# AFNO + SwiGLU block on one core: the first DFT takes rows that are not normalized

## The chip, the cores and the metric

The kernel runs on one core of a Trainium2 chip. The metric is device time in microseconds (us) of the whole program; smaller is better. The kernel before takes 1414.55 us (median of three runs, 1413.67 to 1416.0). Engine names below: PE multiplies matrices (TensorE), DVE is VectorE, ACT is ScalarE, POOL is GpSimd, SP (SyncE) issues most DMA transfers.

## The reference, cut to what matters

```python
x = A_x                                              # 4096 rows of 640
mod = (silu(c) @ w_mod)                              # sa, ca, ga, sb, cb, gb: 640 each
h = layernorm(x) * (1 + ca) + sa
x = x + ga * afno(h)          # rfft2, a two-layer complex MLP by 4 blocks of 160, soft shrink, irfft2
h = layernorm(x) * (1 + cb) + sb
x = x + gb * swiglu(h)        # 640 -> 1728 -> 640
```

The change touches only the first steps: the layer norm of x (each row minus its mean, times its reciprocal deviation) and the first half of the Fourier transform. The factor 1 + ca and the rest of the transform come right behind them.

## The kernel before, in words

The 4096 rows are laid out as 128 partitions (index n1) times 32 (index n2). Eight tiles xa0 to xa7 hold four n2 each: a tile is 128 partitions x 4 rows x 640. The 640 columns are four blocks of 160, each cut into 128 and a remainder of 32.

For each tile the kernel runs these steps. DVE computes statistics (`layer_stats`, L193 and L195), POOL turns them into 1/deviation `rs` (L197, L198) and -mean/deviation `nm` (L406, L407), and ACT (L418) and DVE (L416) together write the normalized rows in place (`ln_apply`). PE then multiplies by the constant DFT matrix `fa` over the partitions (`dft_a`, L439): five matmuls of 128x512 for a tile, one for the 128-wide parts of each row and one for the remainders of all four rows. They go through eight PSUM banks in rotation. ACT (L450, remainders L448) and for the last two tiles also DVE (L446) copy the result back into the same tile (`evac_a`).

The DFT's second half (`stage_b`, L600) needs, for a chunk of frequencies, all 32 n2 on the partitions. So the results are written to a scratch area in DRAM, s10 to s13, and read back as the chunk's tile `g` (`load_g`, L311). For the first chunk, g0, the last two tiles skip the scratch area: `move_g` (L316) copies their pieces from SBUF to SBUF, four transfers of 40 KB for each tile, half of them issued by SP and half by POOL. `moves(t)` is the list of transfers after tile t.

Beside this DVE forms the sum `acc0` of five rows of `w_mod` (`first_scale`, L428 and L430) that becomes the factor `ca1` after a product on PE (`columns`, L327). The first MLP weights w1 and the second ones w2 are each split into a high part (`weights_high`, POOL L281 and ACT L283) and a low part (`weights_low`, DVE L286, and `weights_rest`, POOL L528). The bias b2 is spread over all partitions by three products with ones (L481) and three copies on ACT (L487).

After `stage_b` of the first chunk, ACT and DVE write its parts z (L607, L608) and rz (L630, L640), and PE goes through the MLP: `stage_l1` (L661, L674), then `stage_l2` (L711), which needs the low parts of w1 and w2, the z and rz of each block, and r (L691).

The order on each engine is the order of the code (`manual_schedule`); a tile pool adds the waits. Each transfer reports its end on one of eight semaphores, DMAHW0 to DMAHW7 in the rows of the order below. They are handed out in turn, and a transfer first waits until the one that had its semaphore before has ended.

Of the kernel before, what the change touches and what calls it, by code (L numbers as in the profile page):

```python
# [6 lines left out]
F32 = mybir.dt.float32  # L7
# [6 lines left out]
P = 128  # L14
# [159 lines left out]
def body(tc, x, w1, b1, w2, b2, wg, wu, wd, c, wm, k_fa, k_tb, k_tx, k_bm, k_bx, k_ga, k_ge, k_id, out, dbg=None):  # L174
# [27 lines left out]
    with ExitStack() as top:  # L202
# [35 lines left out]
        with ExitStack() as af:  # L238
# [50 lines left out]
            af.enter_context(tc.manual_schedule())  # L289
            nc.sync.dma_start(fa, k_fa)  # L290
# [45 lines left out]
            stx = ExitStack()  # L336
            xp = stx.enter_context(tc.tile_pool(name="xp", bufs=1, side="right"))
            rp = af.enter_context(tc.tile_pool(name="rp", bufs=1))
            b2t = rp.tile([P, 2, NB, BS], F32, name="b2t")
            with tc.tile_pool(name="sp", bufs=1) as sp:  # L340
                xas = []
                xts = {t: xp.tile([P, 4, D], F32, name=f"xa{t}") for t in (1, 2, 3, 0, 4, 5, 6, 7)}

                def load_x(t):
                    xa = xts[t]
                    if t < 3:
                        for i in range(4):
                            nc.sync.dma_start(xa[:, i, :], xv[:, 4 * t + i, :])
                    else:
                        nc.sync.dma_start(xa, xv[:, 4 * t:4 * t + 4, :])  # L350
                    xas.append(xa)


                def write_s1(t, f):
                    nc.sync.dma_start(s1[f][4 * t:4 * t + 4].rearrange("n r d -> r n d"),
                                      xas[t][(slice(0, 64, 4), slice(64, P, 4), slice(2, P, 4), slice(1, P, 2))[f]])

                for t in range(6):
                    load_x(t)
                wm1 = sp.tile([P, 5, D], F32, name="wm1")  # L360
                stats = {}
                pas = {}
                raws = {}


                def moves(t):
                    if t < 6:
                        write_s1(t, 0)
                    if t < 4:
                        write_s1(t, 1)  # L370
                    if t == 0:
                        load_x(6)
                        nc.sync.dma_start(c5, c)
                    elif t == 1:
                        load_x(7)
                        raws[1] = load_weights(sp, w1, "1")
                    elif t == 2:
                        nc.sync.dma_start(wm1, wm[:, 1])
                    elif t == 3:
                        load_tb(0)  # L380
                        nc.sync.dma_start(b1m, b1[:, 0:8].rearrange("p (r b) -> p r b", r=2))
                        nc.sync.dma_start(b1r, b1[0:64, 8:12])
                        nc.sync.dma_start(b2s[0:1], b2.rearrange("r b o -> (r b o)").unsqueeze(0))
                    elif t == 4:

                        load_g(0, (0, 1))
                        raws[2] = load_weights(rp, w2, "2", (0,))
                    elif t == 5:
                        for f in (2, 3):
                            write_s1(1, f)  # L390
                    elif t == 6:

                        for i in range(4):
                            move_g(0, t, i, (pool, nc.sync)[i // 2])
                        load_g(0, (2,))
                    elif t == 7:
                        for i in range(4):
                            move_g(0, t, i, (pool, nc.sync)[i // 2])


                def ln_stats(t):
                    n = 1 if t < 2 else 4
                    for i in range(0, 4, n):
                        mv, rs = layer_stats(lp, xas[t][:, i:i + n, :], n, f"a{t}_{i}")
                        nm = lp.tile([P, 4], F32, tag="nm", bufs=7, name=f"nm{t}_{i}")
                        pool.tensor_tensor(nm[:, :n], mv[:, :, 0], rs, op=OP.mult)  # L406
                        pool.tensor_tensor(nm[:, :n], nm[:, :n], mone[:, :n], op=OP.mult)  # L407
                        for k in range(n):
                            stats[t, i + k] = (mv[:, k, 0:1], rs[:, k:k + 1], nm[:, k:k + 1])

                def ln_apply(t):
                    xa = xas[t]
                    for i in range(4):
                        mean, rs, nm = stats[t, i]
                        if i >= (4, 2, 2, 3, 2, 3, 2, 1)[t]:
                            dve.tensor_scalar(xa[:, i, :], xa[:, i, :], mean, rs, op0=OP.subtract, op1=OP.mult)  # L416
                        else:
                            act.activation(xa[:, i, :], xa[:, i, :], AF.Identity, bias=nm, scale=rs)  # L418


                b2s = sp.tile([P, 2 * NB * BS], F32, name="b2s")
                pool.memset(b2s, 0.0)
# [32 lines left out]
                for t in range(8):  # L455
                    if t + 2 < 8:
                        ln_stats(t + 2)
# [2081 lines left out]
```

## Time and profile before

| what | value |
|---|---|
| median of 3 runs | 1414.55 us |
| the profiled execution | 1411.32 us, its span 1409.5 us |
| PE busy over the span | 1382.5 us, 98% |
| DVE, ACT, POOL busy | 76%, 54%, 43% |
| first DFT (L439) on PE, first start to last end | 7.98 to 49.30 us |
| first matmul of `stage_b` (L600) | 55.84 us |
| last wait of PE in the first chunk's MLP (L711) ends | 70.20 us |

Times of rows count from the start of the span. A row of the timeline stands for a run of instructions of one line: its start, its length, the engine, line and operation, the tiles out<-in, the count, and in brackets the idle time of the engine before it with what ended that. An f32 matmul is two instructions (x2) for one call in the code. "Idle before" says which engine or transfer came last.

### The profile page before, as it was taken

The page shows a single profiled execution, that of the slowest core. Times are in us where ns is not written, and L with a number is a line of the kernel's source. Part 1 is how long each engine was busy: PE and PEld are TensorE (multiplying, and loading weights), DVE is VectorE, ACT ScalarE, POOL GpSimd, SP SyncE. Part 2 cuts the span into 40 slices and gives each one's busy share as a digit, 9 for nine tenths or more (in the row PEclk, how much of TensorE's full clock was granted, in tenths as well). Part 3 has the DMA queues.
Part 4 walks back from the last instruction along what each step waited for, and adds up shares of the span by engine and source line. Part 5 has one row for each costly group of instructions (what it writes and reads, how often), then busy time and mean ns, then how long its engine had stood idle before and what let it go on. Part 6 is the DMA issues. An engine that isn't in the chain of part 4 may idle for free. (4 is left out here: it accounts for less than half of the span.)

```text
span 1409.5 us, 23754 instructions
## 1 busy us (share of the span) xinstructions
PE 1382.5 (98%) x8410; PEld 1310.7 (93%) x8410; DVE 1067.8 (76%) x1861; ACT 765.0 (54%) x1542; POOL 604.6 (43%) x683
## 2 busy tenths in 40 slices
PE   6899999999999999999999999999999999999998
PEld 2599999967999889899999999999999999999998
DVE  8889888889888888649787668678678757375644
ACT  6879999755555554436454345546164624262341
POOL 5700200157766594326445534447153624042241
PEclk9999999999999999999999999999999999999999
DMA  9876466675998897898877998696998668956634
GB/s 371 310 244 211 157 196 193 203 232 170 327 353 308 308 335 263 293 368 308 308 225 281 375 330 288 236 326 230 375 330 309 217 218 282 350 194 217 199 115 149
DMA packets 171016, 377.34 MB, mean 268 GB/s; under 512 B 22193, under 2 KB 81649, under 8 KB 168882
## 3 DMA queue, kind: packets, MB, share of 16 engines
q1 hardware_dynamic: 161794, 359.28, 73.6%
q0 software_dynamic: 6800, 13.93, 3.1%
q10 hardware_dynamic: 2304, 2.62, 0.5%
q8 instruction: 66, 1.08, 0.3%
q14 instruction: 52, 0.43, 0.1%
HBM read 269.48 MB, written 96.80 MB: 260 GB/s over the span
## 5 line engine op out<-in xcount | busy, mean ns | idle before, releaser
L1442 DVE TENSOR_TENSOR wb<-r,wb 128x768 fp32r<-128x768 f32 (+3 forms) x170 | 170.4, 1013 | 13.5 <-ACT wb L1435 13.3
L2050 PE MATMUL pw<-h,wt 128*128 128x384 f32 x412 | 139.3, 338 | 0.6 <-ACT s_y L2069 0.6
L2052 PE MATMUL pw<-h,wt 128*128 128x384 f32 x412 | 138.3, 336 | 0.0
L2051 PE MATMUL pw<-h,wt 128*128 128x384 f32 x412 | 138.1, 335 | 0.0
L1435 ACT ACTIVATE wb<-r 128x768 fp32r<-128x768 f32 (+3 forms) x168 | 104.5, 639 | 56.3 <-PE pw L2063 41.7
L2351 PE MATMUL pc<-wq,L 128*128 128x320 f32 x846 | 132.7, 309 | 0.9 <-DMA wq<-wqd 0.9
L2110 POOL TENSOR_TENSOR sg<-s_x,sg 128x384 f32<-128x384 f32 x24 | 30.0, 1250 | 234.5 <-DVE s_x L2076 234.5
L2351 PEld LDWEIGHTS pc<-wq,L 128*128 128x128 f32 x846 | 126.3, 188 | 1.1 <-DVE x L2308 1.1
L2130 DVE TENSOR_TENSOR L<-sg,L 128x384 fp32r<-128x384 f32 x144 | 101.0, 725 | 27.7 <-ACT L L2126 27.2
L2069 ACT ACTIVATE s_x<-pw 128x384 f32<-128x384 f32 x52 | 25.6, 492 | 164.2 <-PE pw L2052 162.3
L2050 PE MATMUL pw<-h,wb 128*128 128x384 f32 x312 | 105.0, 336 | 0.0
L2051 PE MATMUL pw<-h,wb 128*128 128x384 f32 x312 | 104.4, 335 | 0.0
L2052 PE MATMUL pw<-h,wb 128*128 128x384 f32 x312 | 104.4, 335 | 0.0
L2121 POOL TENSOR_TENSOR sg<-sg,sg 128x384 f32<-128x384 f32 x72 | 91.9, 1276 | 23.4 <-DVE L L2130 20.0
L1973 PE MATMUL pg<-ht,wb 128*128 128x512 f32 x260 | 101.8, 392 | 0.0
L2351 PE MATMUL pe<-wq,L 128*128 128x320 f32 x648 | 101.7, 309 | 0.0
L1974 PE MATMUL pg<-ht,wb 128*128 128x512 f32 x260 | 101.3, 390 | 0.0
L1975 PE MATMUL pg<-ht,wb 128*128 128x512 f32 x260 | 101.2, 389 | 0.0
L2267 PE MATMUL pd<-wq,a 128*128 128x320 f32 x632 | 96.8, 310 | 0.0
L2351 PEld LDWEIGHTS pe<-wq,L 128*128 128x128 f32 x648 | 96.6, 188 | 0.0
L2267 PEld LDWEIGHTS pd<-wq,a 128*128 128x128 f32 x632 | 93.5, 188 | 0.5
L772 POOL DMA_DIRECT2D s<-co x28 | 15.7, 559 | 175.9 <-ACT co L771 175.9
(317 smaller groups left out, 3914.1 us busy)
## 6 DMA issues: line engine op xcount, KB each, us to landing
wq<-wqd SPq DMA_DIRECT2D x83, 640.0 KB, 6.1
wt<-td SPq DMA_DIRECT2D x103, 512.0 KB, 5.4
hs<-ho SPq DMA_DIRECT2D x52, 512.0 KB, 5.2
h<-hs SPq DMA_DIRECT2D x32, 768.0 KB, 7.9
td<-wt SPq DMA_DIRECT2D x25, 512.0 KB, 6.3
r<-in_B_w_gate_dram SPq DMA_DIRECT2D x24, 384.0 KB, 4.4
r<-in_B_w_up_dram SPq DMA_DIRECT2D x24, 384.0 KB, 4.3
xx<-tt SPq DMA_DIRECT2D x56, 160.0 KB, 3.3
```

The lines of the kernel that those rows point to most:

```text
L1435: def high(ks, e=slice(0, c), copy=lambda o, i: act.activation(o, i, AF.Copy)):
L1442: dve.tensor_tensor(wbs[t, n][:, 1, ks, e], raw[t, n][:, ks, e], f32(wbs[t, n][:, 0, ks, e]), op=OP.subtract)
L1973: mm(b, wh, hh, start=(kk == 0), stop=False)
L1974: mm(b, wh, hl, start=False, stop=False)
L1975: mm(b, wl, hh, start=False, stop=(kk == 4))
L2050: mm(b, w(0, kp), a[:, kp, 0], start=start and kp == 0, stop=False, skip_group_check=not start)
L2051: mm(b, w(0, kp), a[:, kp, 1], start=False, stop=False, skip_group_check=not start)
L2052: mm(b, w(1, kp), a[:, kp, 0], start=False, stop=kp == 1, skip_group_check=not start)
L2121: pool.tensor_tensor(o, x, y, op=op)
L2130: dve.tensor_tensor(o[:, 1], raws[j], f32(o[:, 0]), op=OP.subtract)
L2267: mm(b[:, :320], l, m, start=start and i == 0, stop=stop and i == len(s) - 1)
L2351: mm(o[:, :320], ls[q][:, x, k], w[:, q, y], start=start and q == 0 and n == 0, stop=q == 1 and n == 2, skip_group_check=not start)
```

## The change

For tiles 1 to 6 the rows are no longer normalized before the DFT. Since the DFT runs over the partitions, and each partition has its own mean and deviation, the deviation can be multiplied into the matrix and the mean added behind it. (Line numbers in this section are those of the changed kernel.)

- `scaled` (L489, L491) writes for each row its own matrix wt = fa * rs, 128x128: rows 0 to 2 on ACT, row 3 on POOL (tile 1: all on ACT). The matmul of a row uses wt and the raw row (L527).
- A sixth matmul for each of these tiles, fa times the four columns `nm`, gives what the mean adds: a column of four values for each frequency. ACT copies it to `bt` (`bias_a`, L531), and the copies back from PSUM add it (ACT L543, for two rows of tile 6 DVE L539).
- The remainders of the four rows are still normalized (`rest`, ACT L498, DVE L500): 4x32 elements of each partition and row.
- Tile 0's rows stay normalized on ACT (L480), tile 7's on DVE (L482). Statistics from tile 2 on go in pairs of rows.

Beside that:

- c is loaded by the ACT queue at the start, and its Silu comes ahead of the first row (L421). 14 small matmuls on ones run on PE at the start (`idle(14)`, L422), and 6 instead of 4 behind `columns`.
- b2 is spread by one transfer of 640 KB (L616), behind tb1 on SP, in place of three products and three copies.
- The transfers: `move_g` of tile 6 goes wholly to SP, of tile 7 half to the ACT queue (rows 0 and 2 of the tile) and half to SP. The load of rm2 (the first part of w2) moves behind the writes to s12 and s13 of tile 1.
- The low parts of w1: the first one stands ahead of the last copy of tile 7 on DVE, five ahead of `ca1`, one behind it, and five (`prep1[7:]`) behind the z and rz of block 0.
- The code of `stage_b` and of the copies behind it moves ahead; rz lives in another pool.

```diff
             af.enter_context(tc.manual_schedule())
+            nc.scalar.dma_start(c5, c)
             nc.sync.dma_start(fa, k_fa)
...
                 def moves(t):
                     if t < 6:
                         write_s1(t, 0)
+                    else:
+                        for i in range(4):
+                            move_g(0, t, i, nc.scalar if t == 7 and i % 2 == 0 else nc.sync)
...
                     elif t == 4:
-
                         load_g(0, (0, 1))
-                        raws[2] = load_weights(rp, w2, "2", (0,))
                     elif t == 5:
                         for f in (2, 3):
                             write_s1(1, f)
+                        raws[2] = load_weights(rp, w2, "2", (0,))
                     elif t == 6:
-
-                        for i in range(4):
-                            move_g(0, t, i, (pool, nc.sync)[i // 2])
                         load_g(0, (2,))
-                    elif t == 7:
-                        for i in range(4):
-                            move_g(0, t, i, (pool, nc.sync)[i // 2])
...
+                def scaled(t, *rows):
+                    if t not in wts:
+                        wts[t] = sp.tile([P, 4, P], F32, tag="wt", bufs=2, name=f"wt{t}")
+                    for i in rows:
+                        if t > 1 and i == 3:
+                            pool.tensor_scalar(wts[t][:, i, :], fa, stats[t, i][1], None, op0=OP.mult)
+                        else:
+                            act.activation(wts[t][:, i, :], fa, AF.Copy, scale=stats[t, i][1])
+
+                def rest(t, *rows):
+                    for i in rows:
                         mean, rs, nm = stats[t, i]
...
+                        v = xas[t][:, i, :].rearrange("p (b e) -> p b e", b=NB)[:, :, 128:160]
+                        if i < 2:
+                            act.activation(v, v, AF.Identity, bias=nm, scale=rs)
                         else:
...
+                            dve.tensor_scalar(v, v, mean, rs, op0=OP.subtract, op1=OP.mult)
...
+                    for i in (4, 0, 1, 2, 3) if t == 7 else (0, 1, 2, 3, 4) if t == 0 else (0, 1, 2, 3, 5, 4):
+                        pa = pas[t, i] = bank_a(f"pa{t}_{i}")
+                        if i == 5:
+                            mm(pa[:, 0:4], fa, nms[t], start=True, stop=True)
+                        elif i == 4:
+                            mm(pa, fa, xnr[:, :, :, 128:160], start=True, stop=True)
+                        else:
+                            mm(pa, fa if plain else wts[t][:, i, :], xnr[:, i, :, 0:128], start=True, stop=True)
...
+                def bias_a(t):
+                    bts[t] = sp.tile([P, 4], F32, tag="bt", bufs=3, name=f"bt{t}")
+                    act.activation(bts[t], pas[t, 5][:, 0:4], AF.Copy)
...
+                        elif t == 6 and i % 2:
+                            dve.tensor_scalar(xa[:, i, 0:512], pas[t, i], bts[t][:, i:i + 1], None, op0=OP.add)
+                        elif t == 7 and i == 3:
                             dve.tensor_copy(xa[:, i, 0:512], pas[t, i])
+                        elif t in bts:
+                            act.activation(xa[:, i, 0:512], pas[t, i], AF.Identity, bias=bts[t][:, i:i + 1])
...
+                for t in range(2, 7):
+                    ln_stats(t + 1, A)
+                    rest(t, 2, 3)
+                    ln_stats(t + 1, B)
+                    if t < 6:
+                        scaled(t + 1, 3)
+                    scaled(t, 0, 1)
+                    bias_a(t - 1)
+                    rest(t, 0, 1)
+                    if t == 2:
+                        evac_a(1, 0, 1)
+                    scaled(t, 2)
+                    evac_a(t - 1, *((2, 3) if t == 2 else (0, 1, 2, 3)))
+                    evac_a(t - 1, 4)
                     dft_a(t)
...
+                    moves(t - 1)
...
+                for job in prep1[1:6]:
                     weights_low(*job)
+                dve.tensor_scalar(ca1, pm1[:, 0:5], 1.0, None, op0=OP.add)
...
+                nc.sync.dma_start(b2t.rearrange("p r b o -> p (r b o)"),
+                                  b2.rearrange("r b o -> (r b o)").unsqueeze(0).to_broadcast([P, 2 * NB * BS]))
...
+                weights_low(*prep1[6])
+                evac_b(0, 0)
+                evac_r(0, 0)
+                for job in prep1[7:]:
+                    weights_low(*job)
```

What it does to the order stands below at three places. First SP, from the load of rm2 to the load of rr2 (the second part of w2), before (rm2 is w2's first part, s10 to s13 the scratch areas, g0 the first chunk's tile, xa6 and xa7 the last two tiles; in brackets what a row waits for):

```order
L253 DMA rm2_456<-in_A_w2_dram 128x1280 [waits DMAHW5_49]
L355 DMA s10<-xa5_120 16x4x640 [waits DMAHW6_49,DVE_49,Activation_49]
L355 DMA s12<-xa1_115 32x4x640 [waits DMAHW7_49]
L355 DMA s13<-xa1_115 64x4x640 [waits DMAHW0_49]
L316 DMA g0_453<-xa6_121 4x4x640 [waits DMAHW1_49,Activation_49]
L316 DMA g0_453<-xa6_121 4x4x640 [waits DMAHW2_49,DVE_49]
L311 DMA g0_453<-s10 32x2560 [waits DMAHW6_49,DMAHW3_49]
L316 DMA g0_453<-xa7_122 4x4x640 [waits DMAHW4_49,Activation_49]
L316 DMA g0_453<-xa7_122 4x4x640 [waits DMAHW5_49,DVE_49]
L492 DMA rr2_457<-in_A_w2_dram 128x1280
```

The same stretch of SP after the change:

```order
L416 DMA s12<-xa1_116 32x4x640 [waits DMAHW7_49]
L416 DMA s13<-xa1_116 64x4x640 [waits DMAHW0_49]
L253 DMA rm2_595<-in_A_w2_dram 128x1280 [waits DMAHW1_49]
L317 DMA g0_541<-xa6_122 4x4x640 [waits DMAHW2_49,Activation_49]
L317 DMA g0_541<-xa6_122 4x4x640 [waits DMAHW3_49,DVE_49]
L317 DMA g0_541<-xa6_122 4x4x640 [waits DMAHW4_49]
L317 DMA g0_541<-xa6_122 4x4x640 [waits DMAHW5_49,DVE_49]
L312 DMA g0_541<-s10 32x2560 [waits DMAHW6_49]
L317 DMA g0_541<-xa7_123 4x4x640 [waits DMAHW7_49,Activation_49]
L317 DMA g0_541<-xa7_123 4x4x640 [waits DMAHW0_49,DVE_49]
L608 DMA rr2_596<-in_A_w2_dram 128x1280 [waits DMAHW1_49]
```

Two more moves of tile 6 stand on SP, and the load of rm2 now stands right ahead of all of them, with a wait on DMAHW1.

Second ACT, from the last copies of tile 7 to the first high parts of w1, after the change (before, the copy of xa7's remainders was followed by the high parts at once):

```order
L545 ACTIVATE xa7_123<-pa7_2_624 128x512 [waits PE_49]
L537 ACTIVATE xa7_123<-pa7_4_618 128x4x128 [waits DVE_49,PE_49]
L317 DMA g0_541<-xa7_123 4x4x640 [waits DMAHW1_49,Activation_49]
L317 DMA g0_541<-xa7_123 4x4x640 [waits DMAHW3_49]
L283 ACTIVATE w1a_92<-rm1_362 128x4x128 [waits DMAHW7_49]
L283 ACTIVATE w1b_93<-rm1_362 128x4x128
```

Two moves of tile 7 stand here now, on semaphores DMAHW1 and DMAHW3. In the numbering of the program each comes ahead of SP's transfer with the same semaphore: SP's load of rm2 waits for the count 80 of DMAHW1, which the first of these two moves brings it to, and SP's second move of tile 6 for the count 80 of DMAHW3, which the second one brings it to.

Third DVE, from the second six low parts of w1 (the first six stand ahead of them) to the low part of w2a, before (w1a, w1b, w1c are the parts of w1, pb_0 the PSUM of `stage_b`):

```order
L286 SCALAR_TENSOR_TENSOR w1a<-rm_320,w1a 128x4x128
L286 SCALAR_TENSOR_TENSOR w1b<-rm_320,w1b 128x4x128
L286 SCALAR_TENSOR_TENSOR w1c<-rr_321,w1c 128x4x128
L286 SCALAR_TENSOR_TENSOR w1a<-rm_320,w1a 128x4x32
L286 SCALAR_TENSOR_TENSOR w1b<-rm_320,w1b 128x4x32
L286 SCALAR_TENSOR_TENSOR w1c<-rr_321,w1c 128x4x32
L608 SCALAR_TENSOR_TENSOR z_0_663<-pb_0_646,ca_68,z_0_663 128x2x256
L640 SCALAR_TENSOR_TENSOR rz_666<-pb_4_651,ca_68,rz_666 32x256 x2
L608 SCALAR_TENSOR_TENSOR z_1_671<-pb_1_656,ca_68,z_1_671 128x2x256
L640 SCALAR_TENSOR_TENSOR rz_666<-pb_4_651,ca_68,rz_666 32x256 x2
L286 SCALAR_TENSOR_TENSOR w2a<-rm_456,w2a 128x4x160
```

After, from `ca1` on:

```order
L606 TENSOR_SCALAR ca_68<-pmc 128x5
L286 SCALAR_TENSOR_TENSOR w1a<-rm_362,w1a 128x4x128
L359 SCALAR_TENSOR_TENSOR z_0_734<-pb_0_716,ca_68,z_0_734 128x2x256
L391 SCALAR_TENSOR_TENSOR rz_737<-pb_4_721,ca_68,rz_737 32x256 x2
L286 SCALAR_TENSOR_TENSOR w1b<-rm_362,w1b 128x4x128
L286 SCALAR_TENSOR_TENSOR w1c<-rr_363,w1c 128x4x128
L286 SCALAR_TENSOR_TENSOR w1a<-rm_362,w1a 128x4x32
L286 SCALAR_TENSOR_TENSOR w1b<-rm_362,w1b 128x4x32
L286 SCALAR_TENSOR_TENSOR w1c<-rr_363,w1c 128x4x32
L359 SCALAR_TENSOR_TENSOR z_1_751<-pb_1_726,ca_68,z_1_751 128x2x256
L391 SCALAR_TENSOR_TENSOR rz_737<-pb_4_721,ca_68,rz_737 32x256 x2
L286 SCALAR_TENSOR_TENSOR w2a<-rm_595,w2a 128x4x160
```

Five low parts of w1 have moved from ahead of z of block 0 to between its rz and the z of block 1. From tb1 on (SP) and from the low part of w2a on (the other engines), the two programs have the same instructions in the same order, b2's transfer apart.

452 lines of the change are left out of this document (231 added, 221 removed).

## The prediction

> **What bounds the kernel now.** I read the page's busy times first, then busy time by stretches, then PE's timeline up to 75 us, and only then the other engines in the same stretch.
>
> ```profile
> PE 1382.5 (98%) x8410; PEld 1310.7 (93%) x8410; DVE 1067.8 (76%) x1861; ACT 765.0 (54%) x1542; POOL 604.6 (43%) x683
> ```
> ```profile
> 71.00:1409.50 1338.50, 1327.08 (x8214) 1280.49 (x8212) 1006.84 (x1703) 711.39 (x1449) 558.81 (x603) 1.00 0.77 264
> ```
>
> Behind 71 us PE is busy 1327.08 of 1338.50 us (the first two figures). Nothing that the change touches lies there, and there is almost no idle time to take up a delay. So what the change does to the moment from which PE runs without waits passes to the end nearly one to one. The question is when that moment comes.
>
> ```profile
> 7.98 9.09 PE L439 MATMUL pa<-xa,fa 128*128 128x512 f32 x14 [7.98 <-ACT xa L418]
> 17.78 11.97 PE L439 MATMUL pa<-xa,fa 128*128 128x512 f32 x26 [0.71 <-DVE xa L416]
> 31.56 17.74 PE L439 MATMUL pa<-xa,fa 128*128 128x512 f32 x40 [1.81 <-ACT xa L418]
> ...
> 51.13 2.40 PE L481 MATMUL pb<-b2s,ones 128*128 128x512 f32 x6
> 53.36 1.05 PE L334 MATMUL pz<-ones 128*128 128x128 f32 x8
> 55.84 2.92 PE L600 MATMUL pb<-tb,g 128*128 128x128 f32 x24 [1.43 <-DMA g<-xa]
> ...
> 69.28 0.38 PE L711 MATMUL pc<-w2c,r 128*128 128x320 f32 x1 [1.07 <-DVE r L691]
> 70.20 0.39 PE L711 MATMUL pc<-w2c,r 128*128 128x320 f32 x1 [0.53 <-DVE w2c L286]
> ```
>
> Three things are read here. The DFT ends at 31.56 + 17.74 = 49.30. Then PE has small work until 53.36 + 1.05 = 54.41 and waits 1.43 us, last for a transfer into g. And the last wait, at 70.20, is for DVE: the low part of w2c. Between 55.84 and 70.20 the chain runs over DVE:
>
> ```profile
> 55.13 0.68 DVE L286 SCALAR_TENSOR_TENSOR w1c<-rr,w1c 128x512 fp32r<-128x512 f32 x1
> 55.73 0.28 DVE L286 SCALAR_TENSOR_TENSOR w1a<-rm,w1a 128x128 fp32r<-128x128 f32 x1
> ...
> 57.73 0.75 DVE L608 SCALAR_TENSOR_TENSOR z<-pb,ca,z 128x512 fp32r<-128x512 f32 x1 [1.31 <-ACT z L607]
> 58.87 0.97 DVE L640 SCALAR_TENSOR_TENSOR rz<-pb,ca,rz 32x256 fp32r<-32x256 f32 x2 [0.40 <-ACT rz L630]
> 59.87 0.75 DVE L608 SCALAR_TENSOR_TENSOR z<-pb,ca,z 128x512 fp32r<-128x512 f32 x1
> 60.85 0.98 DVE L640 SCALAR_TENSOR_TENSOR rz<-pb,ca,rz 32x256 fp32r<-32x256 f32 x2 [0.23 <-ACT rz L630]
> 61.86 1.83 DVE L286 SCALAR_TENSOR_TENSOR w2a<-rm,w2a 128x640 fp32r<-128x640 f32 x1
> ...
> 69.16 0.89 DVE L286 SCALAR_TENSOR_TENSOR w2c<-rr,sgn,w2c 128x640 fp32r<-128x640 f32 x1
> ```
>
> From z at 57.73 to 70.05 DVE waits 0.40 and 0.23 us and no more. Whatever is put into that row delays w2c by its length.
>
> **Step 1: the DFT stage ends some 3 us sooner.** PE before needs 17.74 us for the last 20 calls, 0.887 each. Tiles 1 to 7 make 35 such calls, plus six products with four columns. No row shows such a product; the nearest is 24 instructions in 2.92 us in stage_b, 0.24 a pair, and I take 0.2. That is 35 x 0.887 + 6 x 0.2 = 32.2 us. Tile 1 cannot start before its deviations are there:
>
> ```profile
> 11.54 0.21 DVE L195 BATCH_NORM_AGGREGATE mv_a<-st_a 128x2 f32<-128x12 f32 x1
> ...
> 13.73 3.19 DVE L193 BATCH_NORM_STATS2 st_a<-xa 128x6 f32<-128x320 f32 x8
> 16.84 0.41 DVE L195 BATCH_NORM_AGGREGATE mv_a<-st_a 128x2 f32<-128x12 f32 x4
> 17.16 1.08 DVE L416 TENSOR_SCALAR xa<-xa,mv_a,rs_a 128x640 f32<-128x640 f32 x2
> ```
>
> Its second row's mean and variance are there at 11.75; with POOL and one ACT operation behind that (about 2 us) I take 13.9. So PE ends at 13.9 + 32.2 = 46.1, if nothing else holds it: 3.2 us sooner. DVE does not: a tile takes 3.19 + 0.41 and two short operations, about 4.0 us, under PE's 4.6. ACT is close:
>
> ```profile
> 37.05 2.06 ACT L450 ACTIVATE xa<-pa 128x512 f32<-128x512 f32 x4
> 38.95 0.64 ACT L448 ACTIVATE xa<-pa 128x512 f32<-128x512 f32 x1
> 39.43 1.78 ACT L418 ACTIVATE xa<-xa,nm,rs_a 128x640 f32<-128x640 f32 x2
> ...
> 49.34 0.60 ACT L448 ACTIVATE xa<-pa 128x512 f32<-128x512 f32 x1 [0.26 <-PE pa L439]
> ...
> 51.39 0.30 ACT L283 ACTIVATE w1a<-rm 128x128 fp32r<-128x128 f32 x1
> ```
>
> A tile costs it four copies (2.06, or with a bias at most four times 0.8 x 0.89 = 2.85), the remainders' copy (0.64), three 128x128 of wt and two of rest (0.2 to 0.3 each) and bt (about 0.2): 3.9 to 5.2 us, against PE's 4.6. I take PE as the bound and give ACT's upper end to a rival. The products for b2 (2.40), three copies on ACT and the moves that POOL issued cost nothing where they stood, since PE, ACT and POOL waited for g behind them; their going gives nothing.
>
> **Step 2: SP stands still and gives the 3 us back.** SP reaches the load of rm2 early, but that row waits for the semaphore's earlier user, which is ACT's move of tile 7. That move is issued only behind ACT's last copy. With PE 3.2 us sooner, ACT's end at 49.94 becomes 46.5 or so. Until this move has landed, SP issues nothing: not tile 6's four moves, not load_g, not tile 7's two. The transfers have these times (median us from issue to landing, then minimum, median and maximum of all into g):
>
> ```profile
> out_dram<-x ACTq DMA_DIRECT2D x12, 160.0 KB, 1.8
> ```
> ```profile
> g<-s SPq DMA_DIRECT2D x3, 320.0 KB, 4.3
> ...
> g<-xa POOLq DMA_DIRECT2D x4, 40.0 KB, 5.0
> ```
> ```profile
> DMA to landing us min/median/max: 3.4/4.8/5.6
> ```
> ```profile
> 46.65 1.61 SPq L316 DMA_DIRECT2D g<-xa  x2
> 50.14 0.53 SPq L311 DMA_DIRECT2D g<-s  x1
> 50.76 1.20 SPq L316 DMA_DIRECT2D g<-xa  x2
> ```
>
> The move's landing takes 1.8 us (ACT's own queue) to 5.0 us (moves of this size, from POOL). SP's earlier writes will by then have had several us to drain, so I take 2.2: rm2 goes at 48.7. Behind it 0.6 for rm2 and four moves at 0.6 put load_g at 51.7, against 50.14 before; with 4.3 us it lands at 56.0. Tile 7's last move goes at 52.9 and lands at about 55.5. rm2 itself is later too, and ACT splits w2a from it (1.36) ahead of z:
>
> ```profile
> 53.88 1.36 ACT L283 ACTIVATE w2a<-rm 128x640 fp32r<-128x640 f32 x2
> ```
>
> A load of this size took 8.4 us at worst (row further down), which gives 48.7 + 8.4 + 1.4 = 58.5 for z, where step 4 has z at 58.1: covered but for 0.4. Before, stage_b began at 55.84. It will begin near 56.1: **+0.3 us**, with -0.9 (1.8 us for the move, 3.4 for load_g; tile 7's last move then ends it) and +4 (5.0 and 5.6, which give 4.1) as ends. The Trainium skill (DMA: Bandwidth & Descriptors, on arbitration) says that each DMA engine takes packets from its queues in turn, which speaks for the short end: a move on ACT's queue would not wait behind all of SP's. No row here shows it.
>
> **Step 3: five low parts in DVE's chain.** Before, they stood at 54.53 to 56.42, while DVE waited for z anyway. Now they stand between rz and z of the next block: from the rows 0.6 + 0.6 (0.68 less the overlap) and three times 0.2, together 1.85 us. The wait of 0.23 ahead of the second rz goes. That is **+1.6**. If POOL's weight work beside it slows them as it slows w2a (1.83 against 0.89 for w2c of the same size), it is up to +3; but then w2a and w2b come when POOL is further on, and win back as much.
>
> **Step 4: PE runs slow after the wait.** After step 1 PE is done with its six small products near 49 us and has nothing until 56.1: 7 us idle, where before it was 1.43. What idle time does is shown only at the program's start, behind 7.98 us without work:
>
> ```profile
> L439 PE MATMUL pa<-xa,fa x6: 1061/1061/1222, 8.0 to 12.4; 128*128 128x512 f32 x6
> ```
> ```profile
> L439 PE MATMUL pa<-xa,fa x72: 592/592/807, 13.3 to 47.9; 128*128 128x512 f32 x72
> ```
>
> The first matmuls take 1061 ns (median of minimum, median, maximum), those from 13.3 us on 592. If PE begins slow again, stage_b's 24 instructions take 2.92 x 1061/592 = 5.2 us in place of 2.92. The first rz needs 16 of them, +1.55; behind that the low parts of step 3 cover the rest. Ends: 0 and +1.55, and 2.3 if nothing covers it. I take **+1.3**. The Trainium skill (TensorE: Matmul & The Clock Gate, Part 1) has the rule: PE's clock falls to half after an idle window of about 3.4 us and is whole again after about as long at work. By it the 7 us will slow PE here; without it the sum would be +1.9.
>
> The spread of b2 (640 KB) goes behind tb1 and is needed first by DVE's add:
>
> ```profile
> 65.69 0.57 SPq L298 DMA_DIRECT2D tb<-in_k_tb_dram  x1
> ```
> ```profile
> 73.38 0.89 DVE L713 TENSOR_TENSOR tt<-pc,b2t 128x320 f32<-128x320 f32 x2
> ```
> ```profile
> rm<-in_A_w_dram SPq DMA_DIRECT2D x2, 640.0 KB, 8.4
> ```
>
> tb1's issue at 65.69 moves by the 1.6 us that load_g moved, so b2's goes at 67.9 and, taking 8.4 like the first parts of w1 and w2 of the same size, lands at 76.3; the add comes at 73.38 + 3.2 = 76.6. No wait, with little to spare.
>
> The sum: 0.3 + 1.6 + 1.3 = **+3.2 us**. The profiled execution (1411.32 = span 1409.5 + 1.8) is 3.2 under the median; the sum is added to the median: 1414.55 + 3.2 = **1417.75 us**.
>
> **The rivals.**
> - No slow PE. If only step 2 and 3 hold, +0.3 + 1.6 = +1.9: 1416.5. For it: no row shows a slow PE in mid-program. Against: the start does, after as long a pause.
> - It ends faster: the hold on SP does not bite, because the semaphore's count is reached some other way. Then tile 6's moves and load_g go before 46 us, tile 7's moves at 46.5 to 47.7, and g is whole near 50.5, 5.3 us sooner. PE's pause is 2 us. Less step 3: -3.7, so 1410.9. It decides if stage_b starts before 52. Against it stands the order of the rows themselves.
> - A longer hold. ACT binds the DFT (5.2 us for a tile, +0.6 on each of five) or the move lands late: ACT's move comes 2 to 3 us later, and all behind it: +5.2 to +6.2, 1420.3.
> - The change does not do what it says: the DFT ends at 49 as before since ACT's added work is as long as PE's. Then the hold costs its full 3.2 more: +6.4, 1421. I count it with the last one.
>
> **How the numbers follow.** Chances: the sum as it stands 0.55, no slow PE 0.20, a longer hold 0.13, no hold 0.12. About 0.2%, 2.8 us, is what a measurement of this kernel tells from no change. Over +2.8 lie 0.40 of the first case (its terms reach from +2 to +5), a tenth of the second and all of the third: slower 0.55. Within it lie 0.15 and 0.18 of the first two: same 0.33. Faster: 0.12. The range: below 1412.6 most of the case without a hold is left out, and above 1421.5 the worst of the third case (+3.5 of hold, 1.85 and 1.55 make 6.9, 1421.45; the hold's far end of 4 is left out). The likeliest case alone reaches from 1416.5 to 1419.5.
>
> **What would show it.** Step 1: PE's last DFT matmul ends near 46. Step 2: SP's queue shows a gap of some 5 us ahead of rm2, ended by ACT's move of tile 7, and stage_b starts at 56. Step 3: five low parts between rz and z at about 61, and w2c's end 3 us later, near 73. Step 4: L600's instructions at 500 ns in place of 275. The forecast is too slow if stage_b starts before 52, too fast if after 58, and wrong in its frame if PE has new waits behind 80 us.

## The result, and the profile after

| | before | after |
|---|---|---|
| median of 4 runs | 1415.09 us (1413.67 to 1416.0) | 1424.05 us (1422.71 to 1424.53) |
| ratio, with 95% interval | 1 | 1.0063 [1.0045, 1.008] |
| profiled execution, its span | 1411.32, 1409.5 us | 1422.71, 1420.9 us |
| last DFT matmul ends | 49.30 us | 47.76 us |
| first matmul of `stage_b` | 55.84 us | 59.74 us |
| last wait of PE in the first MLP ends | 70.20 us | 76.22 us |

The change makes the kernel 9.0 us slower (median against median). The forecast, 1417.75, was in the right direction and a third of the size (3.2 us); the time lies above the range. The two profiled executions differ by more, 11.4 us, since the one of before is among that kernel's shorter ones.

The busy time of PE in the page of the kernel after, and its granted clock by stretches (columns: PE, PEld, DVE, ACT, POOL busy, the clock, DMA share, GB/s):

```profile
PE 1388.6 (98%) x8448; PEld 1318.8 (93%) x8448; DVE 1065.8 (75%) x1863; ACT 764.1 (54%) x1561; POOL 603.3 (42%) x695
```
```profile
50.00:60.00 10.00, 1.23 (x10) 1.07 (x9) 2.25 (x7) 3.63 (x8) 4.49 (x3) 0.81 0.70 205
60.00:73.00 13.00, 10.78 (x74) 10.09 (x73) 9.27 (x17) 8.11 (x17) 7.05 (x7) 0.88 0.96 331
```

PE's 98% hides the place: from 50 to 60 us it works 1.23 us, and up to 73 us at a clock of 0.88. Its timeline after, at the rows that the prediction named:

```profile
42.16 1.12 PE L525 MATMUL pa<-xa,fa 128*128 128x512 f32 x2 [0.67 <-DVE xa L482]
...
45.78 1.98 PE L527 MATMUL pa<-xa,fa 128*128 128x512 f32 x4 [0.78 <-DVE xa L539]
...
49.39 1.58 PE L335 MATMUL pz<-ones 128*128 128x128 f32 x12
59.74 4.47 PE L351 MATMUL pb<-tb,g 128*128 128x128 f32 x24 [8.77 <-DMA rr<-in_A_w_dram]
...
76.22 0.39 PE L790 MATMUL pc<-w2c,r 128*128 128x320 f32 x1 [0.54 <-DVE w2c L286]
```

The DFT ends at 45.78 + 1.98 = 47.76. Small products follow until 49.39 + 1.58 = 50.97, then an idle time of 8.77 us ahead of `stage_b` (L351 now). The row names rr2's load, the transfer issued last; what L351 reads is tb and g, so the moves into g are what it must wait for (this trace shows no landing of its own for them). Where these moves stand is in the queues of SP and of ACT:

```profile
42.13 1.92 SPq L416 DMA_DIRECT2D s<-xa  x3
50.71 0.34 SPq L253 DMA_DIRECT2D rm<-in_A_w_dram  x1
51.15 2.61 SPq L317 DMA_DIRECT2D g<-xa  x4
53.81 0.53 SPq L312 DMA_DIRECT2D g<-s  x1
54.43 1.20 SPq L317 DMA_DIRECT2D g<-xa  x2
```
```profile
47.80 0.60 ACT L537 ACTIVATE xa<-pa 128x512 f32<-128x512 f32 x1 [0.26 <-PE pa L527]
48.43 1.74 ACTq L317 DMA_DIRECT2D g<-xa  x2
```

SP issues nothing from 44.05 (42.13 + 1.92) to 50.71, when it lets rm2 go 2.28 us behind the issue of ACT's move of tile 7. The last move goes near 55.1 (the second of the two at 54.43), and `stage_b` starts 4.6 us behind that issue.

The loss goes on behind the front. The next rows are the wait of PE for gt, a constant matrix that POOL loads for the inverse transform, POOL's row that issues this load, and SP's transfer (cr) of the same step, before and then after:

```profile
325.24 0.41 PE L1688 MATMUL py<-chl,gt 128*128 128x320 f32 x1 [0.79 <-DVE chl L1678]
...
508.62 0.38 PE L1688 MATMUL py<-chh,gt 128*128 128x320 f32 x1 [1.51 <-DMA gt<-in_k_ga_dram]
```
```profile
504.40 0.64 POOL L1663 DMA_DIRECT2D gt<-in_k_ga_dram  x1
```
```profile
504.44 0.33 SPq L1659 DMA_DIRECT2D cr<-s  x1
```
```profile
331.33 0.41 PE L1751 MATMUL py<-chl,gt 128*128 128x320 f32 x1 [0.82 <-DVE chl L1741]
...
517.04 0.60 PE L1751 MATMUL py<-chh,gt 128*128 128x320 f32 x1 [3.84 <-DMA gt<-in_k_ga_dram]
```
```profile
511.11 0.64 POOL L1726 DMA_DIRECT2D gt<-in_k_ga_dram  x1
```
```profile
510.78 0.33 SPq L1722 DMA_DIRECT2D cr<-s  x1
```

PE is 6.02 us late at 76.22, 6.09 at 331.33 and 8.42 at 517.04. There the pause for gt is 3.84 us in place of 1.51, and the matmul behind it takes 0.60 us in place of 0.38. By matching PE's rows in both traces one by one, the delay is 10.0 us at 520 (by the clock of the trace before) and 10.5 at the end. So some 4.5 us of the difference between these two executions arise after 500 us, at code that the change does not touch.

### The profile page after: what moved, and what is told of

Read it like the earlier page. It is cut to its first block, busy times and chain, and to the rows that moved or that the text cites. A ratio compares the mean times of both kernels' runs of the same rounds, so it can differ in the third digit from the quotient of the medians.

```text
span 1420.9 us, 23871 instructions
## 1 busy us (share of the span) xinstructions
PE 1388.6 (98%) x8448; PEld 1318.8 (93%) x8448; DVE 1065.8 (75%) x1863; ACT 764.1 (54%) x1561; POOL 603.3 (42%) x695
```

## The experiments

Each was timed beside the kernel before on the same chip; "late" is PE's delay against the profile of before at the last matmul that waits for w2c (70.20 there). The medians are against that chip's median of before.

**The hold of SP.** In `e1_pool_moves` POOL issues the two moves that ACT issues in the change, so that rm2's semaphore is not behind ACT's last copy.

```diff
-move_g(0, t, i, nc.scalar if t == 7 and i % 2 == 0 else nc.sync)
+move_g(0, t, i, pool if t == 7 and i % 2 == 0 else nc.sync)
```

> The changed kernel, but tile 7's rows 0 and 2 are moved by POOL's queue, as before the change, so that no transfer on SP shares a semaphore with a move on ACT. Theory (the hold on SP): SP issues rm2 at about 44 us in place of 50.7, load_g(2) at about 48 in place of 53.8, and stage_b starts near 54.3 in place of 59.7. With 3.4 us idle ahead of it PE may or may not run slow. PE's last front wait (for w2c) ends at 70 to 71 in place of 76.2; the time falls by 5 to 6 us against the changed kernel, to about 1415 to 1418. Rival (the transfers into g are late because the DMA engines are full, whatever order SP issues in): stage_b starts at 58 or later, and the time stays within 2 us of 1424.

Measured: 1418.69 us, ratio 1.0037 [1.0019, 1.0055], +5.05 us. SP's queue and PE's rows of this run:

```profile
44.30 0.60 SPq L253 DMA_DIRECT2D rm<-in_A_w_dram  x1
```
```profile
56.49 4.54 PE L351 MATMUL pb<-tb,g 128*128 128x128 f32 x24 [5.19 <-DMA s<-xa]
...
72.98 0.39 PE L790 MATMUL pc<-w2c,r 128*128 128x320 f32 x1 [0.53 <-DVE w2c L286]
```

The hold is gone: rm2 goes at 44.30 in place of 50.71, `stage_b` starts 3.25 us sooner, and PE is 2.8 us late, not 6.0. The front gains 3.2 us and the time 3.9 (+9.0 to +5.05). So the hold is the cause of 3.25 of the 3.9 us by which `stage_b` was late. The start at 56.49 is 2.2 us later than expected and the gain smaller than the 5 to 6 us expected: transfers into g took 6.0 to 6.8 us to land in this run, against 3.4 to 5.6 before. PE still waits 5.19 us and still runs slow behind it (4.54 us for 24 instructions).

**The slow PE at the front.** `e2_warm` keeps PE busy with matmuls on ones until g is there.

```diff
-idle(6)
+idle(44)
```

> The changed kernel with 44 in place of 6 small matmuls on ones behind the column products, so that PE has work until about 59.5 us. Theory (PE ran slow because it had stood idle for 8.8 us): stage_b's 24 instructions take 2.9 us in place of 4.5, and the time falls by 1.5 us. Rival (stage_b's matmuls are slow for another reason, as the transfers beside them): 4.5 us as before and no gain. If a pause of over 3 us ahead of 517 us comes again there (wait for gt), the time behind it stays as in the changed kernel.

Measured: 1422.11 us, 1.006 [1.0037, 1.0082], +8.47 us. PE's rows:

```profile
49.66 10.07 PE L335 MATMUL pz<-ones 128*128 128x128 f32 x88
60.25 2.92 PE L351 MATMUL pb<-tb,g 128*128 128x128 f32 x24 [0.52 <-DMA g<-xa]
...
75.46 0.38 PE L790 MATMUL pc<-w2c,r 128*128 128x320 f32 x1 [0.53 <-DVE w2c L286]
```

`stage_b` takes 2.92 us in place of 4.47: the idle time ahead of it is what made PE slow. But the products themselves last until 59.7, the low parts still stand in the row, and w2c is only 0.8 us sooner. From the start of `stage_b` to the end of the wait for w2c this run needs 15.21 us (75.46 - 60.25), the kernel after 16.48: the slow PE costs 1.27 us up to there. At the time the gain is 0.5 us where 1.5 were expected, and the intervals of this run and of the change overlap: at the time this experiment alone decides nothing.

**The low parts.** `e3_lows` puts all low parts ahead of z and rz again, where DVE waits anyway; `e4_pool_lows` joins this with `e1_pool_moves`.

```diff
+for job in prep1[6:]:
+    weights_low(*job)
-weights_low(*prep1[6])
 evac_b(0, 0)
 evac_r(0, 0)
-for job in prep1[7:]:
-    weights_low(*job)
```

> The changed kernel with the last six low parts of w1 on DVE ahead of z of block 0 again. Theory of the prediction (five low parts stand in DVE's chain and cost their length less 0.23 us): the wait for w2c ends 1.6 us sooner and the time falls by 1.6. Rival from the trace of the changed kernel (they cost 3.2 us there, but w2a and w2b get 1.0 and 0.9 us shorter because POOL is done by then): the gain is 0.5 us, and w2a takes about 1.8 us again.

> Both of the edits: tile 7's moves on POOL's queue and the last six low parts of w1 ahead of z. If the two add up: 0.5 us (rival 1.6) under the run with POOL's moves alone. stage_b starts near 54.3, the wait for w2c ends near 69.5 to 70, and the time is that of the kernel before or 0.5 us under it, 1414 to 1415.5; if the part behind 500 us costs 3 us more whatever the front does, 1417 to 1418.

Measured: `e3_lows` 1421.31 us, 1.0055 [1.0035, 1.0075], +7.67 us; `e4_pool_lows` 1418.15 us, 1.0032 [1.0019, 1.0045], +4.51 us. In the kernel after, the five low parts are these rows of DVE, with w2a behind them:

```profile
64.33 0.97 DVE L391 SCALAR_TENSOR_TENSOR rz<-pb,ca,rz 32x256 fp32r<-32x256 f32 x2 [1.03 <-ACT rz L381]
65.33 0.69 DVE L286 SCALAR_TENSOR_TENSOR w1b<-rm,w1b 128x512 fp32r<-128x512 f32 x1
65.94 2.04 DVE L286 SCALAR_TENSOR_TENSOR w1c<-rr,w1c 128x512 fp32r<-128x512 f32 x1
67.90 0.30 DVE L286 SCALAR_TENSOR_TENSOR w1a<-rm,w1a 128x128 fp32r<-128x128 f32 x1
...
68.32 0.28 DVE L286 SCALAR_TENSOR_TENSOR w1c<-rr,w1c 128x128 fp32r<-128x128 f32 x1
...
70.30 0.82 DVE L286 SCALAR_TENSOR_TENSOR w2a<-rm,w2a 128x640 fp32r<-128x640 f32 x1
```

From 65.33 to 68.60 they take 3.27 us, 2.04 of it one w1c that ran beside POOL's weight work (before, 0.68). w2a then takes 0.82 in place of 1.83, and w2b 0.81 in place of 1.69. From the start of `stage_b` to the end of PE's wait for w2c the kernel after needs 16.48 us, `e3_lows` 13.67 and `e4_pool_lows` 13.46: with the low parts out of the row that stretch is 2.8 to 3.0 us shorter. Neither number expected for `e3_lows` (1.6 and 0.5) has this: w2a and w2b stayed short there too (0.83 and 0.81). But less of it reaches the end: `e3_lows` is 1.7 us sooner at w2c and 1.3 us at the time, inside the intervals. PE's rows in `e3_lows`, and DVE's first add (`tt`) in `e4_pool_lows`:

```profile
60.81 4.84 PE L351 MATMUL pb<-tb,g 128*128 128x128 f32 x24 [9.16 <-DMA s<-xa]
...
74.48 0.39 PE L789 MATMUL pc<-w2c,r 128*128 128x320 f32 x1 [0.46 <-DVE w2c L286]
...
81.26 0.71 PE L789 MATMUL pc<-w2a,h 128*128 128x320 f32 x3 [0.94 <-DVE tt L791]
```
```profile
75.33 0.89 DVE L791 TENSOR_TENSOR tt<-pc,b2t 128x320 f32<-128x320 f32 x2 [3.46 <-DMA s<-xa]
```

Once w2c comes sooner, DVE's first add waits for transfers (3.46 us here), behind the 640 KB for b2, and PE waits for the add: 0.94 us in `e3_lows`, 1.33 in `e4_pool_lows`. With the front of `e4_pool_lows` about level with before (1.5 us early at w2c, 0.1 late behind the add), the time is still 4.51 us over it. So those 4.5 us arise behind the front. In its trace the wait for gt is 4.24 us long, against 1.51 before.

**Kept busy, b2 early, gt early.** `e5_warm_b2` is `e4_pool_lows` with `idle(24)` and the transfer for b2 right behind the load of rr2. In `e6_all` also the load of gt that PE waits for near 508 us comes earlier in POOL's row. `e7_before_gt` and `e8_after_gt` have that last edit alone, in the kernel before and after.

```diff
 def g_in():
+    if r == 10:
+        return
...
 def gated():
+    if r == 10:
+        gtr[10] = take("gt", [P, 2, N1], F32R, 2, "gt10")
+        pool.dma_start(gtr[10].rearrange("p b c -> p (b c)"), k_ga[:, 256 * 10:256 * 10 + 256])
```

> The kernel with POOL's moves and the low parts ahead of z, and two edits more: 24 small matmuls in place of 6 bridge PE's pause until about 55 us, and the 640 KB transfer of b2 goes right behind rr2, not behind tb1. Theory: stage_b starts near 55.3 and takes 2.9 us in place of 4.4, and the add on DVE no longer waits 3.5 us for the write of xa4 behind b2's transfer; the wait for w2c ends near 67.5 us, 2.7 before that of the kernel before. The time falls by 3 us against the run with both edits alone, to 1415 if the pause ahead of 510 us (for gt) is as long there as in that run, and to 1411 if it is as in the kernel before. Rival (PE's slowness or b2 is covered by DVE's chain): less than 1 us.

> The same with the load of gt for row 10 issued by POOL ahead of that row's gated product, some 5 us earlier, into the same buffer. Theory (the pause for gt near 510 us is 1.5 us or about 4 us long, by whether POOL issues it ahead of or behind two transfers of SP; the long one also lets PE run slow for some us): no pause there, granted clock 1.00 throughout, 1407 to 1409, 3 us under the kernel before with the same early load. Rival (the front's gain is lost behind it): no less than the kernel before with the early load.

> The kernel before, with gt of row 10 issued early in the same way. Theory: no pause near 508 us; the runs of the kernel before that show a clock of 0.996 to 0.998 vanish; median 1409.5 to 1411 against some 1413.6, with less spread. Rival (the slow runs come from another place): 1.5 us at most, and the spread stays.

> The changed kernel, with gt of row 10 issued early in the same way. Theory (of the changed kernel's 9 us, 6 are the front's and 3 come from this pause being the long one in each of its runs): 6 us over the kernel before with the early load, so 1415.5 to 1417, 7 us under the changed kernel's 1422 to 1424. Rival (the 3 us come from elsewhere behind the front): it stays 9 us over the kernel before with the early load.

| kernel | median | ratio, 95% | against before |
|---|---|---|---|
| `e5_warm_b2` | 1414.7 | 1.0017 [1.0001, 1.0032] | +1.24 |
| `e6_all` | 1410.8 | 0.9988 [0.9974, 1.0001] | -2.66 |
| `e7_before_gt` | 1410.84 | 0.9985 [0.9971, 1.0] | -2.62 |
| `e8_after_gt` | 1420.98 | 1.0052 [1.0034, 1.007] | +7.52 |

From `e4_pool_lows` to `e5_warm_b2` the end of the front (behind the add) moves by 0.4 us and the time by 3.3. w2c came at 68.81 us, where 67.5 were expected. These are two edits at once; whether a busy PE has such an effect is what the next two pairs test. b2's place was not tested alone. The early gt takes its pause away (none at that row in `e6_all` and `e7_before_gt`) and is worth 2.6 us in the kernel before, at the edge of its interval. `e6_all` gains no more than that, which is the rival of its expectation. In the kernel after it wins only 1.4 (medians against before, +9.0 and +7.5), inside the intervals, where 7 were expected; its trace still shows a wait of 1.50 us for gt, at 516.72.

**Late, with PE busy or idle.** These two kernels add useless work to the kernel before. In `e10_before_later_warm` PE goes on with matmuls on ones, 32 more calls of `idle`; in `e11_before_later_cold` ACT makes ten extra copies and a small product waits for them, so that PE stands still for about as long.

```diff
-idle(4)
+idle(36)
```
```diff
+for _ in range(10):
+    act.activation(gab, acc0, AF.Copy)
+pz = ps.tile([P, P], F32, tag="p3", name="pz")
+mm(pz, ones, gab[:, 0:P], start=True, stop=True)
 for job in prep1:
     weights_low(*job)
```

> The kernel before, with 36 in place of 4 small matmuls ahead of stage_b, so that PE reaches it some 6 us later but never stands idle. It asks whether a later front by itself costs more than its length. Theory A (what the changed kernel loses behind the front, 3 us, comes from PE's slow stretch at the front or from other transfers, not from lateness): the time rises by what stage_b is later, 6 us, less what DVE's chain covers, and the clock is as often 1.00 as in the kernel before. Theory B (lateness moves the later pauses against each other and makes them longer): the time rises by 3 us more than PE's last front wait is later, and the clock falls to 0.996 to 0.998.

> The kernel before, with ten copies on ACT (into a tile that is not used yet) and one small matmul that waits for them ahead of stage_b, so that PE reaches it some 6 us later, behind 7.5 us without work. Theory: stage_b's matmuls run slow (4.5 us in place of 2.9), and PE's last front wait is 7 us later. If PE's slow stretch at the front makes later pauses longer, the time rises by 3 us more than the front, as in the changed kernel; if not, by the front alone, as in the run with the small matmuls.

Measured: 1416.05 us, 1.0015 [1.0002, 1.0027], +2.35 with PE busy; 1423.1 us, 1.0068 [1.005, 1.0087], +9.4 with PE idle. PE's rows and then its windows (PE busy, clock, DMA share, GB/s) with PE busy:

```profile
53.20 8.20 PE L334 MATMUL pz<-ones 128*128 128x128 f32 x72
61.24 2.84 PE L600 MATMUL pb<-tb,g 128*128 128x128 f32 x24
...
73.12 0.39 PE L711 MATMUL pc<-w2c,r 128*128 128x320 f32 x1 [0.50 <-DVE w2c L286]
...
328.18 0.41 PE L1688 MATMUL py<-chl,gt 128*128 128x320 f32 x1 [1.95 <-DVE chl L1678]
```
```profile
50.00:90.00 40.00, 38.98 (x311) 1.00 0.89 317
318.00:345.00 27.00, 25.05 (x115) 1.00 0.70 231
```

And with PE idle:

```profile
61.29 0.80 PE L491 MATMUL pz<-gab,ones 128*128 128x128 f32 x2 [7.18 <-ACT gab L489]
...
75.38 0.39 PE L715 MATMUL pc<-w2c,r 128*128 128x320 f32 x1 [0.53 <-DVE w2c L286]
...
330.54 0.64 PE L1692 MATMUL py<-chl,gt 128*128 128x320 f32 x1 [1.96 <-DVE chl L1682]
```
```profile
50.00:90.00 40.00, 31.63 (x230) 0.91 0.89 315
318.00:345.00 27.00, 25.04 (x105) 0.94 0.70 229
```

Both begin `stage_b` within 0.7 us of each other. At w2c the idle one is 2.26 us behind (75.38 against 73.12); at the time it is 7.05 behind. With PE busy the 2.9 us of delay at the front cost 2.35; with PE idle 5.2 cost 9.4. So with PE idle at the front some 4 to 5 us more are lost later on. The two kernels differ in one thing more, ACT's ten copies. (The execution profiled with PE busy is the longest of its twelve, so these two traces are 5.7 us apart, not 7.05.)

Of the later part, 1.6 us arise at one place in these two traces: the same pause of 1.95 us near 328 us leaves the granted clock at 1.00 in the one and at 0.94 in the other, where the matmul behind it takes 0.64 us in place of 0.41. The clock's own records in the traces show more. In each trace the clock changes only at instants that lie whole multiples of 3.41 us apart, and the slow stretches, at half clock, are 3.41, 6.83 or 10.24 us long. Where these instants lie differs from execution to execution. Here are the two steps of 3.41 us around the pause, with PE busy and then with PE idle at the front:

```profile
326.34:329.75 3.41, 1.57 (x9) 1.00 0.99 342
329.75:333.16 3.41, 3.41 (x17) 1.00 0.94 342
```
```profile
327.15:330.56 3.41, 1.45 (x8) 1.00 1.02 314
330.56:333.97 3.41, 3.41 (x10) 0.50 1.06 394
```

In the second the whole pause lies within one step, in the first the start of a step cuts it. So at this place the fall is explained by where the steps lie, without PE's idle time at the front. The rest of the 5.7 us is 2.3 at the front and 1.8 in small differences behind 500 us.

**Bridging the pause in the kernel after.** `e12_after_warm_gt` is `e8_after_gt` with `idle(44)`.

> The changed kernel with the early load of gt and with 44 small matmuls in place of 6, so that PE does not stand idle ahead of stage_b. Against the run with the early load alone (7.5 us over the kernel before, front 6.5 us late): theory (PE's slow stretch at the front costs more behind it than at it, since later pauses then let PE run slow too): front 5.3 us late, time 4 to 5 us over the kernel before, clock 0.999 or 1.00. Rival (it costs what it costs at the front): 6.3 us over the kernel before, clock 0.998 or lower in half of the runs.

Measured: 1417.47 us, 1.0029 [1.0014, 1.0044], +3.41 us against before, where `e8_after_gt` has +7.52. Windows of PE in `e8_after_gt` and then in `e12_after_warm_gt`:

```profile
50.00:90.00 40.00, 28.79 (x203) 0.87 0.94 328
```
```profile
50.00:90.00 40.00, 36.20 (x288) 1.00 0.90 316
```

The front is 0.7 us sooner behind the add, the time 4.1 us. In the windows of 318 to 345 us, with the same pause of 1.97 and 1.98 us, the clock is 0.94 in the first and 1.00 in the second. The gain goes the same way as in the pair before, though here the intervals still touch, and the same edit without the early gt (`e2_warm`) won 0.5 us.

**All of it.** `e9_all_writes` is `e6_all` with the writes of tile 4 to s12 and s13 ahead of the load of g1, which takes the wait of DVE's first add away.

> The run with all edits (POOL's moves, low parts ahead of z, bridge of small matmuls, b2 behind rr2, early gt), and the writes of xa4 to s12 and s13 ahead of the loads of the second chunk on SP. Theory (DVE's first add waits for the write of xa4, since it takes that tile's place): the add no longer waits, the front is 1.5 us sooner, the time 1409 to 1409.5. Rival (the second chunk's loads, 2 us later, become the wait): PE waits for g1 near 74 us and the time stays at 1411 or rises.

Measured: 1409.95 us, 0.9984 [0.9969, 0.9999], -3.75 us: the best of these kernels, 1.8 us ahead of before at w2c, and the add waits for nothing. Most of the gain is the early gt, which needs no change of the DFT (`e7_before_gt`, -2.62); the 1.1 us more, from another chip, is less than these medians tell apart.

## Why the prediction was right or wrong, point by point

- **Step 1, the DFT 3.2 us sooner:** half right. Tiles 1 to 6 took 4.66 us each (13.50 to 41.48), as forecast. Tile 7 ended 6.3 us behind tile 6 (41.48 to 47.76) in place of 4.4, mostly by the two waits of 0.67 and 0.78 us for DVE in the rows above. The second is for the copies of tile 6, which stand behind the sum `acc0` on DVE:

```profile
42.95 2.12 DVE L509 SCALAR_TENSOR_TENSOR acc<-wm,sc,acc 128x640 f32<-128x640 f32 x2
44.98 1.40 DVE L539 TENSOR_SCALAR xa<-pa,bt 128x512 f32<-128x512 f32 x2
```

  I had compared DVE's sum for a tile with PE's and had not followed its order in the last tile. The DFT ended 1.5 us sooner, not 3.2.
- **Step 2, SP stands still, +0.3:** this is the step that failed, by its size. The mechanism is shown (the gap of 6.7 us ahead of rm2, and `e1_pool_moves`, which removes it), and the landing of ACT's move (2.28 us) was as taken (2.2). But the move went at 48.43, not at 46.5, since the DFT ended 1.7 us later than step 1 had it and ACT's last copy waits for its last matmul. And from the issue of tile 7's last move to `stage_b` it took 4.6 us where the step had taken 2.6 for the landing, with a row for moves of this size at 5.0 us beside it. Together `stage_b` was 3.9 us later in place of 0.3, at the upper end (+4) that the step had kept and the range then left out. (By the step's own terms, 5.0 and 5.6 us, that end is +4.3 against 55.84; its 4.1 counts from the middle of its estimate.)
- **Step 3, five low parts, +1.6:** the mechanism is right, and the size about so once all is counted. In the row they took 3.27 us, the upper bound that the step named (+3, one w1c slowed beside POOL). But w2a and w2b came when POOL was further on and took 1.89 us less than before, which the step had named too; 1.4 are left. Against the kernel without them in the row (`e3_lows`) they cost 2.8 us up to w2c, and behind w2c the wait of DVE's first add hides part of it.
- **Step 4, a slow PE, +1.3:** right at its place. `stage_b` took 4.47 us in place of 2.92, +1.55, and up to w2c the slow PE cost 1.27 us (`e2_warm`). The instructions of L351 in the kernel after, as a group (minimum, median, maximum in ns; 275 median before, by the same view):

```profile
L351 PE MATMUL pb<-tb,g x24: 274/421/554, 59.7 to 63.9; 128*128 128x128 f32 x24
```

  The Trainium skill (TensorE: Matmul & The Clock Gate, Part 1) has the clock fall to half behind an idle window of about 3.4 us; the 8.77 us here agree with it, and `e2_warm`, where the idle time is filled and the matmuls take 2.92 us, agrees too.
- **"Passes to the end nearly one to one":** wrong, and no step had a term for it. The prediction read the 11.4 us of idle time behind 71 us only as too little to take up a delay and put at nothing that pauses there can grow: the front was 6.0 us late, the time 9.0. With `e4_pool_lows` the front was level with before and the time 4.5 us over it. The prediction's own sign for this, new waits of PE behind 80 us, appeared at 517 us.
- **The spread of b2, no wait:** right in the kernel after (0.31 us), but only because w2c was late there. With w2c 1.7 and 7.5 us sooner (`e3_lows`, `e4_pool_lows`) DVE's first add waited 3.06 and 3.46 us.
- **The rivals:** "a longer hold" (1420.3, chance 0.13) was nearest in its mechanism, and still 3.7 us too low. "No slow PE" and "no hold" fell by the rows above.

In numbers: `stage_b` is 3.9 us late (step 2, forecast 0.3), and from its start to the end of the wait for w2c the kernel takes 16.48 us in place of 14.36, +2.1 (steps 3 and 4, forecast 2.9). That makes the 6.0 us of the front, so the miss at the front is step 2's alone. The other 3.0 of the 9.0 us come later. With the hold, the low parts in the row and the idle time of PE all taken away, and b2 sooner (`e5_warm_b2`), 1.24 of the 9.0 us are left.

Two parts of what comes later can be seen in the traces. One is the wait for gt. POOL's issue, at 511.11, stands after the change behind SP's transfer for the same step (510.78), and before the change 0.04 us ahead of it (504.40 against 504.44); it lands 5.80 us behind its issue after, 4.09 before. The other traces without the early gt agree: ahead of SP's transfer it lands in 4.0 to 4.2 us (`e2_warm`, `e5_warm_b2`), behind it in 5.6 to 6.2 (`e1_pool_moves`, `e3_lows`, `e4_pool_lows`, `e10_before_later_warm`, `e11_before_later_cold`). The long wait stands there with PE idle at the front and with PE busy (`e10_before_later_warm`, 3.56 us). The other part is the clock at half behind long pauses, 516.97 to 520.38 us in the kernel after. That kernels whose PE stands idle at the front lose 4 to 5 us more behind it is shown by one pair on one chip (with ten copies of ACT as a second difference) and made likely by the other pair; `e2_warm` does not show it. By what path the idle time would act so much later stays open.

## What to carry to other kernels

A semaphore that transfers of several queues use in turn ties these queues together: where a transfer is moved to another engine, look up who used its semaphore before, and when that engine will come to issue it. An engine's mean work for a tile says nothing on the last tile: follow the order on every engine to the last copy, since the moves and all that waits for them start there. An idle time of PE can cost more than its length: here 1.55 us in the 24 instructions behind it, and filling it with products of no use was worth 4.1 us in one kernel (`e12_after_warm_gt`) and 0.5, inside the intervals, in another (`e2_warm`). And a stretch in which PE is busy 1327 of 1338 us can still grow: one of its pauses was 2.3 us longer where two queues issued in the other order.

## What the runs showed of the hardware that was not expected

- The Trainium skill (TensorE: Matmul & The Clock Gate, Part 1) has the clock fall behind an idle window of about 3.4 us. Here a pause of 1.92 to 1.98 us near 325 us was followed by half clock for 3.41 us in `e1_pool_moves`, `e3_lows`, `e7_before_gt`, `e8_after_gt` and `e11_before_later_cold`, and by full clock in `e5_warm_b2`, `e6_all`, `e9_all_writes`, `e10_before_later_warm` and `e12_after_warm_gt`; the measurement decides. What tells these apart is the step of 3.41 us (from one possible change of the clock to the next) that holds the pause: in the first five PE is busy 1.44 to 1.49 us of it, in the other five 1.54 to 2.30. This is not the whole rule: the clock also fell at 69.05 us in `e6_all` and at 71.08 in `e7_before_gt`, behind steps in which PE was busy 0.53 of the time.
- The mean granted clock of a whole run goes with its time: the profiled runs at 1.000 of before, `e5_warm_b2` and `e9_all_writes` have spans of 1406.8 to 1409.5 us, those at 1.000 with a late front (`e12_after_warm_gt`, `e2_warm`) 1414.8 and 1415.3 us, and those at 0.994 to 0.996 of the change, `e1_pool_moves`, `e3_lows`, `e8_after_gt` and `e11_before_later_cold` 1419.2 to 1422.7. The mean holds the front's own slow stretch too: the 6.83 us at half clock in the kernel after take 0.0024 off it. The row of PEclk on the page shows 9 throughout in the kernel after; the slow stretches show only in windows of 40 us and less.
- The move of 40 KB that ACT's queue issued had released rm2 2.28 us behind its issue, while moves of the same size issued by POOL in the kernel before took 5.0 (median). Other transfers were under way beside them, so this does not compare the two queues alone.
